# Experts of a routed MLP: steps of 256 tokens with the weights still in layer 1, in place of blocks of 128

## The chip, the cores and the metric

The kernel runs on one core of one Trainium2 chip. The metric is the device time of one execution in microseconds (us), less is better. A profiled execution gives the trace; its times count from the first instruction. PE is TensorE's matmuls, PEld its weight loads, DVE is VectorE, ACT is ScalarE, POOL is GpSimd, SP is SyncE, which issues DMAs.

## The reference

```python
# attention with a memory term, 4 x 8 heads x 576 tokens x 64     -> x (2304, 512)
x = moe(x, w_in, w_out)          # relu(x @ w_in)**2 @ w_out, d_ff 2048
xn, en = x / |x|, emb / |emb|
logits = xn @ en.T / tau         # 8 experts
expert_idx = argmax(logits, axis=1);  gate_w = softmax(logits)[expert_idx]
for e in range(8):
    h = np.maximum(x[mask_e] @ w1[e], 0.0)        # 512 -> 1024
    out[mask_e] = gate_w[mask_e] * (h @ w2[e])    # 1024 -> 512
```

On its inputs the experts 0 to 7 get 466, 171, 106, 0, 676, 436, 0 and 449 tokens, worked out from the reference itself.

## The kernel before

All products are made of three float32r matmuls: each operand is split in a high part (`...h`, an ACT copy) and the rest (`...l`, a DVE subtraction), and hi\*hi + lo\*hi + hi\*lo is summed in PSUM.

The program runs attention, with the first half of the MLP woven in; then the second half of the MLP in 9 chunks of 256 tokens (`Mlp.layer1`: weights still, x moving, 12 matmuls 256 wide; `Mlp.layer2`: 6 matmuls 512 wide; chunks in the order 8, 0, 1, ..., 7). Behind each chunk DVE and PE route its tokens (`Mlp.route`): the expert's number, the rank within the expert (`R.lj`: rank modulo 128 and block number), a one-hot tile `R.L` that POOL makes from the rank. After four chunks `first_block` names the expert with most tokens so far as the first; the experts run in the order 4, 5, 7, 0, 1, 2. It gathers its first 128 tokens, of which the places come from small matmuls into `tab0`, and turns them on PE (`xT0`), so that the experts can begin before the routing is done.

`tables` then works out, on DVE with one row of matmuls on PE (`tab`), the token of each row of each block (`T.idxg`), where to store it (`T.idxs`), and words of bits in `T.meta` by which the engines branch: `odd` (which of two weight buffers a block uses), `change` (the expert changes), `more` (there is another expert to load). Its second part, the gates (norms, an exponential, three products `rg`, and 18 matmuls `tg`), is only needed where results are stored.

`experts` runs blocks of 128 tokens: 18 for sure, up to 25 behind branches; 21 run here. Each has two arms in the code, one for each weight buffer (`Wh[slot]`, `Wl[slot]`). In an arm the order of PE, ACT and DVE is as written:

- `layer1`: x still, 24 matmuls with 512 weights moving; ACT's Relu brings h to SBUF
- `turn_h` twice: 4 PE transposes of h, then hi and lo (`hh`, `hl`)
- `layer2`: 24 matmuls, 512 wide, into `y`; `turn_x`: 4 transposes of the next block's gathered tokens `xg`, then hi and lo
- `own` and `ahead`: pieces of a new expert's weights are split in hi and lo (ACT, DVE), in blocks next to a change of expert
- behind the arm: SP's loads of later weights, POOL's gather for block s + 2, DVE's scaling by the gate, POOL's scatter (`store`)

Of the kernel before, what the change touches and what calls it, by code (L numbers as in the profile page):

```python
# [9 lines left out]
F32 = DT.float32  # L10
F32R = DT.float32r
# [19 lines left out]
NBLK = 25  # L31
NSURE = 18
# [26 lines left out]
TURN0 = 5  # L59
# [554 lines left out]
class Mlp:  # L614
# [158 lines left out]
    def routing(self, c, late, emb, tau):  # L773
# [8 lines left out]
        self.sq = c.tile([128, DM], BF16, name="sq")  # L782
# [18 lines left out]
    def route(self, cc, x2):  # L801
# [51 lines left out]
        V.tensor_reduce(rk, t16, AX.X, ALU.add)  # L853
        ri = c.tile([128, 2, 2], I32, name="ri", tag="ri")
# [17 lines left out]
    def first_block(self):  # L872
# [36 lines left out]
        for sl in spans:  # L909
            V.scalar_tensor_tensor(b0[:, sl], R.lj[:, 1, sl], 0.0, R.O[:, sl, 0], ALU.is_equal, ALU.mult)  # L910
            V.tensor_scalar_mul(rhs[:, sl, 0], b0[:, sl], R.iotap)
            V.tensor_tensor(rhs[:, sl, 1], b0[:, sl], R.iotat[:, sl, 0], ALU.mult)
        tab = R.ps.tile([128, 512], F32, name="tab0", tag="r")
        tiles = [t for sl in spans for t in range(sl.start, sl.stop)]
        for t in tiles:
            nc.tensor.matmul(tab[:, :2], R.L[:, t], rhs[:, t], start=t == tiles[0], stop=t == tiles[-1])
        p1 = c.tile([128, 1], F32, name="p1")
        V.tensor_scalar(p1, tab[:, 0:1], -1.0, None, ALU.add)
        idx = c.tile([128, 1], I32, name="idx0")
        V.scalar_tensor_tensor(idx, tab[:, 1:2], 128.0, p1, ALU.mult, ALU.add)  # L920
        m = len(tiles) * 128
        nc.gpsimd.indirect_dma_start(sh.xg[0], None, sh.x2d[:m], IO(ap=idx, axis=0), bounds_check=m - 1, oob_is_err=False)
        for _ in range(TURN0):
            yield
        pt = self.psr.tile([128, 512], F32, name="xt", tag="xt", bufs=2)
        for kc in range(4):
            nc.tensor.transpose(pt[:, kc * 128:kc * 128 + 128], sh.xg[0][:, kc * 128:kc * 128 + 128], sh.ident)
        sh.xT0 = [c.tile([128, DM], F32R, name=n) for n in ("xT0h", "xT0l")]
        split(nc, pt, *sh.xT0, nc.scalar, nc.vector)
        yield  # L930

# [30 lines left out]
def routing_setup(tc, sh, c):  # L962
# [20 lines left out]
    R.iotat = c.tile([128, NTT, NBLK], BF16, name="iotat")  # L983
    for a, n, base in ((0, NTT - 2, 2), (NTT - 2, 2, 0)):
        nc.gpsimd.iota(R.iotat[:, a:a + n], [[1, n], [0, NBLK]], base=base, channel_multiplier=0,
                       allow_small_or_imprecise_dtypes=True)

    R.two = c.tile([128, NBLK], I32, name="two")
    nc.gpsimd.iota(R.two, [[1, NBLK]], base=126, channel_multiplier=0)
# [8 lines left out]
def tables(ctx, tc, sh):  # L998
# [5 lines left out]
    T.idxg = c.tile([128, NBLK], I32, name="idxg")  # L1004
    T.idxs = c.tile([128, NBLK], I32, name="idxs")
    T.gate = c.tile([128, NBLK], F32, name="gate")
    T.meta = c.tile([128, NBLK + 4], I32, name="meta")
# [7 lines left out]
    V.tensor_scalar(ci, cnt[:, :E], 127.0, None, ALU.add)  # L1015
    V.tensor_scalar(ci, ci, 7, None, ALU.arith_shift_right)
# [4 lines left out]
    for t in cum:  # L1021
# [15 lines left out]
    V.tensor_tensor(sb, sb, R.lj[:, 1], ALU.add)  # L1037
    Bk = st.tile([128, NTT, NBLK], BF16, name="Bk")
    V.tensor_tensor(Bk, R.iota128[:, :NBLK].unsqueeze(1).to_broadcast([128, NTT, NBLK]),
                    sb.unsqueeze(2).to_broadcast([128, NTT, NBLK]), ALU.is_equal)  # L1040
    rg = st.tile([128, NTT, 3, NBLK], BF16, name="rg")
    rhs = rg[:, :, :2]
    V.tensor_scalar_mul(rhs[:, :, 0], Bk, R.iotap)
    V.tensor_tensor(rhs[:, :, 1], Bk, R.iotat, ALU.mult)
    tab = pst.tile([128, 512], F32, name="tab", tag="r")
    for i in range(NTT):
        nc.tensor.matmul(tab[:, :2 * NBLK], R.L[:, i], rhs[:, i].rearrange("p a b -> p (a b)"),
                         start=i == 0, stop=i == NTT - 1)
    P1 = st.tile([128, NBLK], F32, name="P1")
    V.tensor_copy(P1, tab[:, :NBLK])  # L1050
    idx = st.tile([128, NBLK], F32, name="idx")
    V.scalar_tensor_tensor(idx, tab[:, NBLK:2 * NBLK], 128.0, P1, ALU.mult, ALU.add)
    first = V.tensor_scalar(T.idxg, idx, -1.0, 0.0, ALU.add, ALU.max)
    for s in range(1, 2):
        nc.gpsimd.indirect_dma_start(sh.xg[s], None, sh.x2d, IO(ap=T.idxg[:, s:s + 1], axis=0),
                                     bounds_check=NT - 1, oob_is_err=False)
    with tc.issue_after(first.ins):
        ge = st.tile([128, NBLK, E], F32, name="ge")
        V.tensor_tensor(ge, R.iota128[:, :NBLK].unsqueeze(2).to_broadcast([128, NBLK, E]),
                        cend.unsqueeze(1).to_broadcast([128, NBLK, E]), ALU.is_ge)  # L1060
        ex = st.tile([128, NBLK], F32, name="ex")
# [5 lines left out]
        V.tensor_tensor(ge, ge, used.unsqueeze(1).to_broadcast([128, NBLK, E]), ALU.mult)  # L1067
        at = st.tile([128, NBLK], F32, name="at")
# [3 lines left out]
        V.tensor_tensor(ge, at.unsqueeze(2).to_broadcast([128, NBLK, E]), rank.unsqueeze(1).to_broadcast([128, NBLK, E]),  # L1072
                        ALU.is_equal)
        flags = st.tile([128, 3, NBLK], F32, name="flags")
        V.memset(flags[:, :, 0], 0.0)
        more = st.tile([128, NBLK], F32, name="more")
        V.tensor_reduce(more, ge, AX.X, ALU.add)
        V.tensor_tensor(ge, ge, R.iota128[:, :E].unsqueeze(1).to_broadcast([128, NBLK, E]), ALU.mult)
        nx = st.tile([128, NBLK], F32, name="nx")
        V.tensor_reduce(nx, ge, AX.X, ALU.add)  # L1080
        e8 = st.tile([128, NBLK], I32, name="e8")
        V.tensor_scalar(e8, nx, R.e0, None, ALU.add)
        V.tensor_scalar(T.meta[:, :NBLK], e8, E - 1, None, ALU.bitwise_and)
        lt = st.tile([128, NBLK], F32, name="lt")
        V.tensor_scalar(lt, ex, 7.5, None, ALU.is_lt)
        V.tensor_tensor(flags[:, 1, 1:], at[:, 1:], at[:, :NBLK - 1], ALU.not_equal)
# [5 lines left out]
        V.tensor_tensor(flags, flags, R.two.bitcast(F32).unsqueeze(1).to_broadcast([128, 3, NBLK]), ALU.mult)  # L1092
        words = st.tile([128, 4], F32, name="words")
        V.tensor_reduce(words[:, :3], flags, AX.X, ALU.add)
        V.tensor_copy(words[:, 3:], cend[:, E - 1:E])
        last = V.tensor_copy(T.meta[:, NBLK:], words)
        neg = st.tile([128, NBLK], F32, name="neg")
        V.tensor_scalar(neg, idx, 0.0, BIG, ALU.is_equal, ALU.mult)
        wrap = st.tile([128, NBLK], F32, name="wrap")
# [4 lines left out]
    with tc.issue_after(last.ins):  # L1104
# [29 lines left out]
def experts(tc, sh, gates, w1, w2, out):
    nc = tc.nc
    T = sh.T
    with ExitStack() as ctx:
        st = ctx.enter_context(tc.tile_pool(name="est", bufs=1, reuse_waits="tile"))
        psh = [sh.psm.tile([128, 512], F32, name=f"psh{j}", tag="y", bufs=2) for j in range(2)]
        pst = [sh.psm.tile([128, 512], F32, name="pst0", tag="L1", bufs=1)]  # L1140
        pst += [sh.psr.tile([128, 512], F32, name=f"pst{j}", tag="xt", bufs=2) for j in range(1, 3)]
        psy = [sh.psr.tile([128, 512], F32, name=f"psy{j}", tag="y", bufs=2) for j in range(2)]
        ident = sh.ident
# [15 lines left out]
        new_h = ring(1, "h", [128, F], F32)
        new_hh = ring(2, "hh", [128, 512], F32R)  # L1160
        new_hl = ring(2, "hl", [128, 512], F32R)
        spare = sh.x1[NCH - 1].rearrange("p a b -> p (a b)")
        new_psh = ring(2, "psh", None, None, psh)
        new_pst = ring(3, "pst", None, None, pst)
        new_psy = ring(2, "psy", None, None, psy)

        xg, xT, hb = {}, {}, {}

        def gather(s):
            if s >= NBLK:  # L1170
                return
            t = sh.xg[s % 2]
            nc.gpsimd.indirect_dma_start(t, None, sh.x2d, IO(ap=T.idxg[:, s:s + 1], axis=0),  # L1173
                                         bounds_check=NT - 1, oob_is_err=False)
            xg[s] = t

        def turn_x(s):
            if s >= NBLK:
                return
            t = xg.pop(s)  # L1180
            pt = new_pst()
            for kc in range(4):
                nc.tensor.transpose(pt[:, kc * 128:kc * 128 + 128], t[:, kc * 128:kc * 128 + 128], ident)
# [255 lines left out]
```

## Time and profile before

| what | value |
|---|---|
| time, median of 3 runs (lowest to highest) | 978.58 us (978.37 to 980.16) |
| the profiled execution | 976.67 us, of which the span of its instructions is 974.7 us |
| mean granted TensorE clock | 0.982 |
| PE busy | 924.9 us, 95% of the span |
| DVE, ACT, POOL busy | 615.6, 553.8, 278.6 us |

Matmuls overlap: the length of one in a timeline is longer than the distance between the starts of two, and the distance is what a matmul costs. So costs on PE are read from start to start. The expert stage runs from 691.92 us, the first matmul of block 0, to the last matmul at 966.39 us.

### The profile page before, as it was taken

What the parts mean: (1) busy time and instruction counts of PE and PEld (TensorE: products, weight loads), DVE (VectorE), ACT (ScalarE), POOL (GpSimd) and SP (SyncE); (2) the same over time, 40 slices, a digit from 0 to 9 for tenths busy, and PEclk for the clock granted to TensorE, in tenths of its full rate; (3) what the DMA queues carried; (4) which work ended last, traced back from release to release, by engine and by line L of the source; (5) the groups of instructions that cost most, each with busy time, mean ns of one, the idle gap of its engine ahead of it and who ended that gap; (6) DMA issues with size and microseconds to landing.
All of it is one profiled execution on the core that took longest, in us unless ns stands there. A gap on an engine that the chain in (4) does not pass through costs nothing. (4 is left out here: it accounts for less than half of the span.)

```text
span 974.7 us, 19052 instructions
## 1 busy us (share of the span) xinstructions
PE 924.9 (95%) x5864; PEld 772.3 (79%) x5864; DVE 615.6 (63%) x1741; ACT 553.8 (57%) x1425; POOL 278.6 (29%) x346
## 2 busy tenths in 40 slices
PE   7887798899999999999999999999989999999996
PEld 6666675688888888898888988898777878887875
DVE  4797768656676765488517778888642444444364
ACT  4676767677676766576655555664422434444353
POOL 4364554533333443101111112441412111111121
PEclk8999989899999999999999999999999999999998
DMA  6676655454444430254311112421061342425160
GB/s 165 148 177 149 156 138 143 99 127 94 117 95 115 95 85 2 67 171 154 109 44 44 64 46 92 158 66 44 23 218 46 92 154 85 173 73 185 66 204 28
DMA packets 106779, 105.10 MB, mean 108 GB/s; under 512 B 65967, under 2 KB 76207, under 8 KB 106624
## 3 DMA queue, kind: packets, MB, share of 16 engines
q1 hardware_dynamic: 101200, 90.17, 33.2%
q0 software_dynamic: 4224, 12.89, 3.9%
q8 instruction: 58, 0.95, 0.4%
q14 instruction: 97, 0.79, 0.3%
q10 hardware_dynamic: 1200, 0.30, 0.1%
HBM read 70.01 MB, written 14.43 MB: 87 GB/s over the span
## 5 line engine op out<-in xcount | busy, mean ns | idle before, releaser
L680 PE MATMUL ps<-xh,Wh 128*128 128x256 f32 x416 | 119.7, 288 | 0.0
L392 POOL TENSOR_SCALAR A<-A,sm,g 128x512 f32<-128x512 f32 (+4 forms) x108 | 75.4, 706 | 153.3 <-DVE sm L455 60.9
L680 PE MATMUL ps<-xl,Wh 128*128 128x256 f32 x416 | 118.3, 284 | 0.9 <-DVE xl L654 0.9
L680 PE MATMUL ps<-xh,Wl 128*128 128x256 f32 x416 | 118.1, 284 | 0.0
L714 PE MATMUL y<-Wh,gh 128*128 128x512 f32 x288 | 115.3, 400 | 0.1
L716 PE MATMUL y<-Wh,gl 128*128 128x512 f32 x288 | 113.6, 394 | 0.0
L715 PE MATMUL y<-Wl,gh 128*128 128x512 f32 x288 | 113.4, 394 | 0.0
L446 ACT ACTIVATE A<-A,nm 128x256 f32<-128x256 f32 (+2 forms) x144 | 80.3, 558 | 37.8 <-DVE nm L438 36.8
L690 DVE TENSOR_TENSOR gl<-r,gh 128x256 fp32r<-128x256 f32 x144 | 69.5, 483 | 46.2 <-ACT gh L689 41.7
L684 ACT ACTIVATE r<-ps 128x256 f32<-128x256 f32 x144 | 54.8, 380 | 76.5 <-PE ps L680 73.1
L438 DVE CUSTOM_DVE_ANT_0 A<-ps,mask 64x256 f32<-64x256 f32 (+4 forms) x160 | 75.5, 473 | 33.7 <-PE ps L431 30.9
L109 DVE TENSOR_TENSOR hl<-pst,hh 128x512 fp32r<-128x512 f32 x42 | 29.0, 691 | 104.4 <-ACTq L1215 93.6
L680 PEld LDWEIGHTS ps<-xh,Wh 128*128 128x128 f32 x416 | 79.7, 192 | 4.9 <-issue 1.9
L680 PEld LDWEIGHTS ps<-xl,Wh 128*128 128x128 f32 x416 | 79.8, 192 | 3.8 <-DVE xl L654 1.1
L680 PEld LDWEIGHTS ps<-xh,Wl 128*128 128x128 f32 x416 | 79.9, 192 | 0.0
L689 ACT CAST gh<-r 128x256 fp32r<-128x256 f32 x144 | 58.4, 405 | 37.6 <-PE y L715 35.5
L1308 POOL DMA_INDIRECT out_dram<-x,idxs x21 | 21.2, 1011 | 197.1 <-DVE x L1307 149.4
L1250 PE MATMUL psy<-Wh,hh 128*128 128x512 f32 x168 | 70.2, 418 | 0.0
L1252 PE MATMUL psy<-Wh,hl 128*128 128x512 f32 x168 | 66.8, 398 | 0.4 <-DVEq L1215 0.4
L108 ACT CAST Wh<-x 128x512 fp32r<-128x512 f32 x96 | 55.0, 618 | 20.5 <-SPq L1297 7.9
L1251 PE MATMUL psy<-Wl,hh 128*128 128x512 f32 x168 | 66.4, 395 | 0.0
L716 PEld LDWEIGHTS y<-Wh,gl 128*128 128x128 f32 x288 | 54.1, 188 | 13.6 <-DVE gl L690 0.7
(333 smaller groups left out, 2426.6 us busy)
## 6 DMA issues: line engine op xcount, KB each, us to landing
x<-in_moe_w_dram SPq DMA_DIRECT2D x48, 512.0 KB, 3.8
raw<-in_moe_w_in_dram SPq DMA_DIRECT2D x16, 512.0 KB, 4.1
raw<-in_moe_w_out_dram SPq DMA_DIRECT2D x16, 512.0 KB, 4.0
ks<-hk SPq DMA_DIRECT2D x60, 128.0 KB, 2.4
x2d<-x SPq DMA_DIRECT2D x18, 256.0 KB, 2.0
kn<-in_k_dram SPq DMA_DIRECT2D x32, 128.0 KB, 2.8
vn<-in_v_dram SPq DMA_DIRECT2D x32, 128.0 KB, 2.7
x2p<-x SPq DMA_DIRECT2D x16, 256.0 KB, 2.4
```

What stands on the lines that cost most here:

```text
L392: nc.gpsimd.tensor_scalar(A, A, a, b, ALU.mult, ALU.mult)
L438: nc.vector.tensor_tensor_reduce(A[rows, a:n], tiles[j][rows, :w], mask[rows, end - w:end], -1.0, 3e38, ALU.add, ALU.min, nm[rows, j:j + 1])
L446: nc.scalar.activation(A[:, a:a + w], src, AF.Exp, bias=nm[:, 0:1], scale=sign, accum_out=sm[:, i:i + 1])
L680: nc.tensor.matmul(ps[:, :CH], a, b, start=n == 0, stop=n == len(ops) - 1)
L689: self.later(3, "act", lambda: nc.scalar.copy(gh, r))
L690: self.later(3, "dve", lambda: nc.vector.tensor_tensor(gl, r, gh.bitcast(F32), ALU.subtract))
L714: nc.tensor.matmul(y, gh[:, sl], wh, start=first, stop=False)
L715: nc.tensor.matmul(y, gh[:, sl], wl, start=False, stop=False)
L716: nc.tensor.matmul(y, gl[:, sl], wh, start=False, stop=last)
L1250: nc.tensor.matmul(y, hh[:, sl], a, start=n == 0 and kc == 0, stop=False)
L1251: nc.tensor.matmul(y, hh[:, sl], b, start=False, stop=False)
L1252: nc.tensor.matmul(y, hl[:, sl], a, start=False, stop=n == 1 and kc == 3)
```

## The change

- A step of 256 tokens takes the place of two blocks; there are at most 17 steps, 9 for sure. Their tables have 34 columns (halves of steps) where there were 25.
- Layer 1 holds 128 x 128 of the weights still and moves the step's 256 tokens: 96 matmuls 256 wide a step, in four groups `g` of 256 hidden units. Its result comes out turned, so h isn't transposed; ACT makes `hh` from PSUM by Relu and DVE `hl` from PSUM by max and subtraction.
- Layer 2 runs the two halves of 128 tokens apart, each 6 matmuls a group. From step 1 on, the second half stands in a branch that PE alone takes: past it when the step's second half holds no token (a new word of bits, `half`).
- The order in a step: layer 1 of group 0 and 1, layer 2 of 0 and 1, layer 1 of 2 and 3, layer 2 of 2, 8 transposes of the next step's tokens, layer 2 of 3.
- Step 0 needs 256 tokens of the first expert ahead of the tables: `first_block` gathers and turns a second half after 7 chunks (`SEEN`). `R.hole` leaves ranks free if fewer than 256 of them were seen.
- The gates' second part on DVE is issued ahead of step 0 in place of behind block 1, and `sq`, an output that nobody reads, is put in a part of `x1[8]`.

The diff, cut to its core:

```diff
-NBLK = 25
-NSURE = 18
+NST = 17
+NHB = 2 * NST
+NSURE = 9
+SEEN = 7
...
-        self.sq = c.tile([128, DM], BF16, name="sq")
+        self.sq = self.sh.x1[NCH - 1].rearrange("p a b -> p (a b)")[:, DM:2 * DM]
...
         V.tensor_reduce(rk, t16, AX.X, ALU.add)
+        if n >= SEEN:
+            V.scalar_tensor_tensor(rk, O[:, :, 0], R.hole[:, 0:1], rk, ALU.mult, ALU.add)
...
+        fetch(0)
         for _ in range(TURN0):
             yield
...
+        turn(0)
+        while R.count < SEEN:
+            yield
+        cnt = R.ps.tile([128, 512], F32, name="cnt", tag="r")
+        nc.tensor.matmul(cnt[:, :E], R.ones, R.Osum[:, SEEN - 1], start=True, stop=True)
+        V.tensor_scalar(R.hole[:, 0:1], cnt[:, 0:1], -1.0, float(CH), ALU.mult, ALU.add)
+        V.tensor_scalar_max(R.hole[:, 0:1], R.hole[:, 0:1], 0.0)
+        fetch(1)
+        for _ in range(TURN1):
+            yield
+        turn(1)
         yield
...
+            def layer1(g):
+                ps = new_bank().rearrange("p (a b) -> p a b", a=2)
+                for a in range(2):
+                    sl = slice((2 * g + a) * 128, (2 * g + a) * 128 + 128)
+                    for kc in range(4):
+                        for j, (w, x) in enumerate(((Wh, hi), (Wh, lo), (Wl, hi))):
+                            nc.tensor.matmul(ps[:, a], w[kc][:, sl], x[:, kc], start=kc + j == 0, stop=kc + j == 5)
+                hh, hl = hT[g] = new_hh(), new_hl()
+                nc.scalar.activation(hh, ps, AF.Relu)
+                nc.vector.scalar_tensor_tensor(hl, ps, 0.0, hh.bitcast(F32), ALU.max, ALU.subtract)
+
+            def layer2(g):
+                hh, hl = hT[g]
+                for h in range(2):
+                    with tc.If(bit(words["half"], s) < 1) if s and h else nullcontext():
+                        half(g, h, hh, hl)
...
+            own(4)
+            layer1(0)
+            own(5)
+            layer1(1)
+            own(6)
+            layer2(0)
+            own(7)
+            layer2(1)
...
+            ahead(0)
+            layer1(2)
+            ahead(1)
+            layer1(3)
+            ahead(2)
+            layer2(2)
+            if s + 1 < NST:
+                for h in range(2):
+                    turned(nc, sh, pst[h], h)
+            ahead(3)
+            layer2(3)
...
         load(range(8), 0)
...
+        next(gates)
+        block(0)
```

**The order, place 1: PE in an arm.** The first rows are an arm of before, in the middle of its layer 2 (`psy` is y, `pst` a bank for transposes, line 1229 turns h).

```order
L1250 MATMUL psy_9291<-Wh_4_5678,hh_9295 128x512
L1251 MATMUL psy_9291<-Wl_4_5686,hh_9295 128x512
L1252 MATMUL psy_9291<-Wh_4_5678,hl_9297 128x512
L1229 MATMUL pst_9288<-ident,h_9294 128x128 x4
L1250 MATMUL psy_9291<-Wh_5_5679,hh_9295 128x512
```

Here are the rows of the change, in a step's layer 2 of group 2, at the branch around the second half (`psy_9341`).

```order
L1253 COMPARE_AND_BRANCH
L1261 MATMUL psy_9341<-Wh_6_5680,hh_9343 128x512
L1262 MATMUL psy_9341<-Wl_6_5688,hh_9343 128x512
L1263 MATMUL psy_9341<-Wh_6_5680,hl_9345 128x512
L1261 MATMUL psy_9341<-Wh_6_5680,hh_9343 128x512
L1262 MATMUL psy_9341<-Wl_6_5688,hh_9343 128x512
L1263 MATMUL psy_9341<-Wh_6_5680,hl_9345 128x512
L1253 UNCONDITIONAL_BRANCH
L1253 UNCONDITIONAL_BRANCH [waits PE_49]
L961 MATMUL pst_9338<-ident,xg_6592 128x128 [waits DMASW4_49]
```

The transposes of h are gone; the two that end a branch are the end of the body and the way past it, and the way past waits for PE's own work.

**The order, place 2: DVE where the gates' second part stands.** In before that is the end of block 1 (the second of its arms is shown): the lo part of block 2's tokens stands first, the gates (lines 936 and on) behind it:

```order
L109 TENSOR_TENSOR xT0l<-pst_9289,xT0h 128x512
L1221 COMPARE_AND_BRANCH
L109 TENSOR_TENSOR Wl_3_82<-x_3_93,Wh_3_74 128x512
L1221 UNCONDITIONAL_BRANCH x2
L1283 UNCONDITIONAL_BRANCH
L936 TENSOR_SCALAR sq<-ss 128x18
L937 TENSOR_SCALAR sq<-sq 128x18
```

In the change that is the end of step 0. `xTl` is the lo part of step 1's tokens, written in two halves, and the rows around it are the gates:

```order
L1153 CAST gp<-gt 128x18
L1154 TENSOR_TENSOR gr<-gt,gp 128x18
L1159 TENSOR_TENSOR rg<-Bk,gp 128x18x34
L1155 CAST gp<-gr 128x18
L111 TENSOR_TENSOR xTl<-pst_9338,xTh 128x4x128
L1235 COMPARE_AND_BRANCH
L111 TENSOR_TENSOR Wl_3_5685<-x_3_93,Wh_3_5677 128x512 x2
L1235 UNCONDITIONAL_BRANCH x2
L1156 TENSOR_TENSOR gr<-gr,gp 128x18
L1159 TENSOR_TENSOR rg<-Bk,gp 128x18x34
L1157 CAST gp<-gr 128x18
L111 TENSOR_TENSOR xTl<-pst_9339,xTh 128x4x128
```

The gates have moved ahead of both halves of `xTl`, which step 1's second matmul reads.

**The order, place 3: PE in the second half of the MLP, one MLP step after the seventh chunk was routed.** Before:

```order
L680 MATMUL ps<-xh_8736,Wl_0_5682 128x256
L714 MATMUL y<-Wh_7_5681,gh 128x512
L715 MATMUL y<-Wl_7_5689,gh 128x512
L716 MATMUL y<-Wh_7_5681,gl 128x512
L714 MATMUL y<-Wh_7_5681,gh 128x512
```

In the change 14 pairs of a weight load and a matmul into `tab` stand there, of which the first is shown; `L` is the one-hot tile of POOL:

```order
L682 MATMUL ps<-xh_8739,Wl_0_5682 128x256
L716 MATMUL y<-Wh_7_5681,gh 128x512
L717 MATMUL y<-Wl_7_5689,gh 128x512
L926 LDWEIGHTS L
L926 MATMUL tab_8844<-rhs_8043,L 128x2
```

The MLP's third matmul of that group now stands behind those 14.

## Rows read from the trace of the kernel before

**Rows 1.** The page, busy time of PE

```profile
PE 924.9 (95%) x5864; PEld 772.3 (79%) x5864; DVE 615.6 (63%) x1741; ACT 553.8 (57%) x1425; POOL 278.6 (29%) x346
```

**Rows 2.** Windows: length; busy PE, PEld, DVE, ACT, POOL; granted clock, DMA share, GB/s

```profile
691.92:752.49 60.57, 56.72 (x306) 45.07 (x305) 29.15 (x115) 15.28 (x28) 12.37 (x12) 0.97 0.32 111
752.49:966.62 214.13, 212.43 (x1021) 172.51 (x1019) 97.99 (x149) 93.70 (x165) 37.92 (x35) 1.00 0.36 121
...
706.76:710.17 3.41, 1.30 (x8) 1.18 (x9) 2.30 (x10) 0.59 (x1) 1.36 (x2) 1.00 0.58 154
710.17:713.58 3.41, 3.41 (x10) 2.63 (x9) 2.21 (x9) 0.41 (x1) 0.63 (x1) 0.50 0.42 105
```

**Rows 3.** Timeline of PE, block 4: start, length, what

```profile
752.49 0.40 PE L1240 MATMUL psh<-Wh,xT0h 128*128 128x512 f32 x1
...
756.46 0.60 PE L1229 MATMUL pst<-ident,h 128*128 128x128 f32 x4
...
757.13 0.39 PE L1240 MATMUL psh<-Wh,xT0h 128*128 128x512 f32 x1
```

**Rows 4.** Timeline of PE, one step of the MLP's second half

```profile
561.80 0.28 PE L680 MATMUL ps<-Wh,Wh 128*128 128x256 f32 x1
...
563.21 0.40 PE L714 MATMUL y<-Wh,gh 128*128 128x512 f32 x1
...
564.62 0.28 PE L680 MATMUL ps<-Wh,Wh 128*128 128x256 f32 x1
```

**Rows 5.** PE's waits from 740 to 967 us: total, times, longest

```profile
PE pst L1229 <- ACT h L1259: 1.7, 3, 0.8
```

**Rows 6.** PE's waits from 691 to 740 us, the second longest

```profile
PE psh L1240 <- DVE lj L858: 0.8, 1, 0.8
```

**Rows 7.** Timeline, the tables during block 0: PE, then DVE

```profile
697.93 0.18 PE L1013 MATMUL cnt<-Osum,ones 128*128 128x8 bf16 x1
...
703.80 0.61 PE L1047 MATMUL tab<-rg,L 128*128 128x50 bf16 x18
...
708.87 0.66 PE L1183 MATMUL pst<-ident,xg 128*128 128x128 f32 x4 [2.25 <-DMA xg<-x2d,idxg]
...
702.29 0.63 DVE L1039 TENSOR_TENSOR Bk<-iota,sb 128x450 bf16<-128x450 f32 x1
...
704.89 0.18 DVE L1053 TENSOR_SCALAR idxg<-idx 128x25 int32<-128x25 f32 x1
...
712.53 0.17 DVE L1096 CAST meta<-words 128x4 int32<-128x4 f32 x1
```

**Rows 8.** Timeline of DVE, the gates' second part, first and last

```profile
724.65 0.18 DVE L936 TENSOR_SCALAR sq<-ss 128x18 int32<-128x18 int32 x1 [0.34 <-issue]
...
730.25 1.70 DVE L1123 TENSOR_TENSOR rg<-Bk,gp 128x450 bf16<-128x450 bf16 x3
```

**Rows 9.** Timeline, routing of the seventh chunk: PE, and POOL's `L`

```profile
666.16 0.18 PE L845 MATMUL pr<-O,tri 128*128 128x16 bf16 x1 [1.19 <-DVE O L840]
...
668.25 1.18 POOL L860 TENSOR_SCALAR L<-iota,lj 128x128 bf16<-128x128 f32 x2 [2.26 <-DVE lj L858]
```

**Rows 10.** Groups by line from 740 to 960 us, DVE and ACT

```profile
L109 DVE TENSOR_TENSOR hl<-pst,hh 128x512 fp32r<-128x512 f32 x35 | 24.2, 692 | 91.8 <-ACTq L1215 82.8 <-ACT hh L108 8.5 <-issue 0.6
...
L1259 ACT ACTIVATE h<-psh 128x512 f32<-128x512 f32 x18 | 10.8, 598 | 51.7 <-PE psh L1240 46.1 <-issue 5.1 <-ACTq L1221 0.5
```

**Rows 11.** Branches of PE's sequencer: ns min/median/max, first and last start

```profile
L1283 PEldq COMPARE_BRANCH  x2: 68/129/190, 749.6 to 750.0; - x2
...
L1283 PEldq COMPARE_BRANCH  x31: 68/208/358, 710.1 to 951.8; - x31
...
L1334 PEldq COMPARE_BRANCH  x5: 67/73/3432, 925.9 to 968.4; - x5
```

**Rows 12.** Timeline, the end: PE, POOL

```profile
966.39 0.39 PE L1252 MATMUL psy<-Wh,hl 128*128 128x512 f32 x1
...
967.85 1.01 POOL L1308 DMA_INDIRECT out_dram<-x,idxs  x1 [10.16 <-DVE x L1307]
```

More of the change, by code (lines that the diff above doesn't have):

```diff
@@ L56 @@
 STRICT, BUSY = 9, {-5: 14, 0: 12, 2: 6}
-TURN0 = 5
+TURN0, TURN1 = 5, 3
 ONPE = (NCH - 2,)
@@ L917, in first_block, with fetch @@
[L917 to L922, printed above, removed]
+        sh.xT = [c.tile([128, 4, CH], F32R, name=n) for n in ("xTh", "xTl")]
+        def fetch(half):
+            n = R.count - 1
+            spans = [slice(0, 2 * n), slice(NTT - 2, NTT)]
+            for sl in spans:
+                V.scalar_tensor_tensor(b0[:, sl], R.lj[:, 1, sl], float(half), R.O[:, sl, 0], ALU.is_equal, ALU.mult)
+                V.tensor_scalar_mul(rhs[:, sl, 0], b0[:, sl], R.iotap)
+                V.tensor_tensor(rhs[:, sl, 1], b0[:, sl], R.iotat[:, sl], ALU.mult)
+            tab = R.ps.tile([128, 512], F32, name="tab0", tag="r")
+            tiles = [t for sl in spans for t in range(sl.start, sl.stop)]
+            for t in tiles:
+                nc.tensor.matmul(tab[:, :2], R.L[:, t], rhs[:, t], start=t == tiles[0], stop=t == tiles[-1])
+            p1 = c.tile([128, 1], F32, name=f"p1_{half}")
+            V.tensor_scalar(p1, tab[:, 0:1], -1.0, None, ALU.add)
+            at = c.tile([128, 1], F32, name=f"at_{half}")
+            V.scalar_tensor_tensor(at, tab[:, 1:2], 128.0, p1, ALU.mult, ALU.add)
+            idx = c.tile([128, 1], I32, name=f"idx_{half}")
+            V.tensor_scalar_max(idx, at, 0.0)
+            m = len(tiles) * 128
+            nc.gpsimd.indirect_dma_start(sh.xg[half], None, sh.x2d[:m], IO(ap=idx, axis=0), bounds_check=m - 1,
+                                         oob_is_err=False)
@@ L923, in first_block, with turn @@
+        def turn(half):
+            pt = self.psr.tile([128, 512], F32, name="xt", tag="xt", bufs=2)
+            turned(nc, sh, pt, half)
+        fetch(0)
         for _ in range(TURN0):
             yield
[L925 to L928, printed above, removed]
@@ L1053, in tables @@
+    V.tensor_copy(P1, tab[:, :NHB])
+    idx = st.tile([128, NHB], F32, name="idx")
+    V.scalar_tensor_tensor(idx, tab[:, NHB:2 * NHB], 128.0, P1, ALU.mult, ALU.add)
     first = V.tensor_scalar(T.idxg, idx, -1.0, 0.0, ALU.add, ALU.max)
-    for s in range(1, 2):
-        nc.gpsimd.indirect_dma_start(sh.xg[s], None, sh.x2d, IO(ap=T.idxg[:, s:s + 1], axis=0),
+    for n in range(2):
+        nc.gpsimd.indirect_dma_start(sh.xg[n], None, sh.x2d, IO(ap=T.idxg[:, 2 + n:3 + n], axis=0),
                                      bounds_check=NT - 1, oob_is_err=False)
@@ L1278, in block, with arms @@
+            ahead(3)
+            layer2(3)
+        def arms(s, flag, *does):
+            kept = [list(r) for r in rings]
+            with tc.If(bit(words[flag], s) < 1) as cmp, tc.manual_schedule(engines=IN_ORDER | {ENG.PE}):
+                does[0]()
+            for r, was in zip(rings, kept):
+                r[:] = was
+            with cmp.Else(), tc.manual_schedule(engines=IN_ORDER | {ENG.PE}):
+                does[1]()
         def block(s):
-            kept = [list(r) for r in rings], dict(xg), dict(xT)
@@ L1293, in block @@
-            if s + 1 < NBLK:
-                with tc.If(bit(more, s + 1) > 0):
+                body(0, 0)
+                words["odd"] = word(0, [ENG.PE, ENG.Activation, ENG.DVE])
+                words["change"] = word(1, [ENG.Activation, ENG.DVE])
+                words["more"] = word(2, [ENG.SP])
+                words["half"] = word(3, [ENG.PE])
+            else:
+                arms(s, "odd", lambda: body(s, 0), lambda: body(s, 1))
+            if s + 1 < NST:
+                with tc.If(bit(words["more"], s + 1) > 0):
@@ L1315, in experts @@
-        change = word(1, [ENG.Activation, ENG.DVE])
-        more = word(2, [ENG.SP])
-        y = block(0)
+        next(gates)
+        block(0)
         with tc.manual_schedule(engines={ENG.PE, *IN_ORDER}):
-            nc.scalar.copy(room(0), y)
-            y = block(1)
-            nc.scalar.copy(room(1), y)
-            next(gates)
-            odd = word(0, [ENG.PE, ENG.Activation, ENG.DVE])
-            y = block(2)
-            next(gates, None)
-        store(0, room(0))
-        store(1, room(1))
@@ L1334, in experts @@
         with ExitStack() as ifs:
-            for s in range(NSURE, NBLK):
+            for s in range(NSURE, NST):
                 ifs.enter_context(tc.If(nbv > s))
-                store(s, block(s))
+                block(s)
+                store(s, y)
 @with_exitstack
@@ L1404, in tile_kernel @@
             pass
+        for _ in sh.R.first:
+            pass
     gates = tables(ctx, tc, sh)
```

287 lines of the change are left out of this document (107 added, 180 removed).

## Prediction

> **What bounds the kernel.** I read the page first: PE is busy 95% of the span [rows 1], so time can be won where PE does less or waits less, and elsewhere only for a wait of PE. The order before the second half of the MLP is the same in both kernels, so I looked at the expert stage and the MLP chunks just ahead of it. Windows cut the expert stage in two [rows 2]: blocks 0 to 3 took 60.57 us, the other 17 took 214.13 us, 12.6 each. In the latter PE waits 1.7 us in all [rows 5]; it is a stream of matmuls. The timeline gives their price, start to start [rows 3]: 17 matmuls 512 wide from 752.49 to 756.46, 0.234 us each; 4 transposes and the matmul behind them 0.67, so a group of transposes costs 0.44. A block is 48 x 0.234 + 3 x 0.44 = 12.5. In blocks 0 to 3, PE also does routing work and waits: 0.8 us for the load of `once` behind DVE [rows 6], 2.25 us for block 1's gather behind the tables [rows 7], and then the granted clock is at its lower level (0.50) for 3.4 us while PE is busy throughout [rows 2], which costs half of that, 1.7.
>
> **A step.** The new layer 1 has the operands and shape of the MLP's: 12 matmuls 256 wide took 1.41 us, 6 of 512 took 1.41 [rows 4]. So a step has 8 x 1.41 for layer 1, 8 x 1.41 for layer 2, and 8 transposes in a row, 0.8 by 2 x 0.36 and a little behind them: 23.4 us for 256 tokens, where two blocks take 24.9. The whole gain of a step is the 16 transposes of h.
>
> Padding takes some back. The experts' counts (676, 436, 449, 466, 171, 106) make 6+4+4+4+2+1 = 21 blocks, and 3+2+2+2+1+1 = 11 steps. Only the last step (106 tokens) has an empty second half, where PE saves 24 wide matmuls, 5.6 us; its layer 1 moves all 256 columns. That step is 17.7 us, and about 1.8 more, since at each of four skips the sequencer waits for PE's own last matmul (an estimate: the length of a matmul, 0.4, less nothing hidden, four times). Steps 2 to 10: 9 x 23.4 - 5.6 + 1.8 = 206.5 against 214.1: **7.6 us less**. In that I put new waits in these steps at nothing. What hides them: hl(g) has 2.8 us (one group of the next layer 1) and more until layer 2 reads it, and needs 0.60 on ACT and 0.69 on DVE [rows 10]; a piece of new weights in front of it is 2 x 0.69 on DVE, and a step that splits eight pieces has 11 us of them plus 6 us of its own work in 23. Without that cover a step next to a change would lose what before lost, some 0.6, at five changes 3 us.
>
> **Steps 0 and 1.** Step 0 begins like block 0. The routing of the last chunk sets the start up to `cnt`, which I leave at 697.9 [rows 7]. From there PE has layer 1 of group 1, layer 2 of group 0 and six single matmuls until `tab`: 2.8 + 2.8 + 1.1, at 704.7. DVE took 5.9 us from `cnt` to `tab` in before; in the change it has one hl more (0.69), tables 34/25 as wide (Bk 0.63 becomes 0.86, the two behind it gain about as much), and loses an idle half microsecond: 704.7 too. `tab` ends 0.65 later at 705.4, 1.0 after that of before.
>
> Behind it PE has 9 wide matmuls, two groups of layer 1, one of layer 2, the transposes and the last group of layer 2: 2.1 + 5.6 + 2.8 + 0.8 + 2.8 = 14.1, and would begin step 1 at 719.6. The gather is hidden: its tokens were there 4.0 us after `idxg` began [rows 7], the second gather adds one issue, about 1.1, and 10.5 us pass until the transposes. So both waits of before go (0.8 and 2.25).
>
> But DVE gets late. It owes, from `tab`'s end: idxg (0.6), the rest of the tables, 712.7 - 705.1 = 7.6 in before with 1.2 of idle time and two splits of 0.6 inside [rows 7], so about 5 now that most are 17 wide; hl(2); the gates' second part, 724.65 to 731.95 = 7.3 [rows 8], of which the three products cost 0.77 each at 34 columns, one of them behind the last split; the load of `once` (0.6) and four skipped branches (0.3 each); hl(3); and the two halves of xTl, the second of them behind it all. With waits of some half microsecond for ACT's exponential: 0.6 + 5 + 0.5 + 0.7 + 7.1 + 0.6 + 1.2 + 0.7 + 1.4 = 17.8, so 723.2; by going through the instructions one by one I come to 722.8. **PE stands from 719.7 to 722.8, 3.1 us**, at the second matmul of step 1. Bounds: none if DVE overlaps as it does in places (two chains interleaved run at 0.1 an instruction); 5 if each wait is paid. A wait of 2.25 brought the lower clock before, so I add 1.6 for it; bounds 0 and 3.4 (two such stretches). Step 1 then takes 23.4, and `tg` 0.9. Step 2 begins at 722.7 + 23.4 + 1.6 + 0.9 = 748.6 against 752.49: **3.9 us less**.
>
> **The MLP chunk in front.** The second half's places (`tab0`, place 3 of the order) need `L` of the seventh chunk. That was made by POOL at 668.25 to 669.43 [rows 9], and DVE's two instructions for `hole` come before it, about 0.3. PE is at `tab0` some 12 x 0.118 + 2 x 0.234 + 0.3 after `pr` at 666.16: 668.4. It waits there until about 669.8, and the 14 small matmuls, `cnt` and four transposes (0.44) cost 0.9. **2.3 us more**; bounds 0.9 (no wait) and 3.
>
> **The end.** In before the scatter is issued 1.1 us after the last matmul's end [rows 12]. Now two results are scaled (0.7 each) and two scatters issued (1.0 each) behind it: **1.2 us more**, bounds 0 and 2.
>
> **PE's branches.** Ten steps have four branches on PE each, and each step jumps over one arm. Before, a jump over an arm took the sequencer 0.07 to 0.36 us [rows 11], and nothing of it reached PE: the sequencer was at block 3's end at 749.6, 2.9 us before block 4's first matmul [rows 3, 11]. An arm had 60 matmuls, now it has 152. The last branch of before, over four blocks of two arms, took 3.43 us [rows 11]. I take 0.5 us for all, and 0 to 34 (ten jumps of 3.43) as bounds, the row of jumps over one arm being far nearer.
>
> [...]
>
> **Sum.** 7.6 + 3.9 - 2.3 - 1.2 - 0.5 = 7.5 us less than the profiled 976.67, which is 1.9 below the median of the runs; on that median 978.58 - 7.5 = 971. A difference of 0.2%, 2 us, is about what this measurement can tell.
>
> **Rivals.**
> - *DVE isn't late, or the clock holds.* For it: half of my chain are short instructions that overlap. Against it: the order of place 2. It gives back 3 to 5 us: 966. Chance 0.15.
> - *The skips don't work and waits come back.* The empty half is one of 22; were it not skipped, 3.8 us, and with new waits next to the changes of expert (3) the rest of the gain is gone: 978. Against it: the changes had 1.7 us of waits [rows 5] with four splits in a row, now two. Between forecast and that, or within 2 us of 978.6: 0.24, half of it within.
> - *Jumps reach PE* (the other side). At each step PE's sequencer stands 3.43 us, and its lead of 2.9 is used up by four branches in a step: each about 0.1 to compare and 0.2 to 0.3 to jump back. Then up to 3.4 us of ten steps show: 971 + 34 = 1005 at most. It decides from 0.75 us a step, 7.5 in all; with half of the lead gone it is 2 us a step: 991. For it: the 3.43 us row. Against it: the lead is made anew in each group of wide matmuls. Chance 0.13.
> [...]
>
> **Numbers.** Forecast 971, its own range 967 to 975, chance 0.48. The range for 8 in 10 takes in the second and half of the third case: 964 to 981. Faster by more than 0.2%: 0.48 + 0.15 + 0.12 = 0.75; same 0.12; slower 0.13.
>
> **What the next profile shows.** Right: step to step 23.4 us without idle PE from step 2 on; no gather wait in step 0; PE idle about 3 us at the first layer 1 of step 1 with xTl's subtraction as the one that ends it, and a lower clock behind it; PE idle over 1 us at `tab0`. Wrong: idle PE or longer spacing at line 1253's branches or at each step's start (jumps); idle PE at layer 2 for hl in steps 2 to 10; steps far from 23.4, which would mean that matmuls 256 wide cost more here than in the MLP.

## The result and the profile after

The changed kernel takes **984.34 us** (median of 12 runs, 982.62 to 990.59) against 978.48 us of before, timed beside it (12 runs, 977.35 to 980.16): a ratio of 1.0069, 95% interval 1.0052 to 1.0087. It is slower; the forecast was 971, so 13.3 us are missing. The profiled execution took 984.24 us, its span 982.5.

Windows, cut at the first matmul of each step, show where (columns as in [rows 2]):

```profile
696.02:723.81 27.79, 27.20 (x201) 24.63 (x199) 21.34 (x101) 6.42 (x13) 10.27 (x9) 1.00 0.39 137
723.81:749.39 25.58, 24.27 (x171) 21.80 (x170) 6.29 (x11) 4.06 (x7) 0.02 (x1) 1.00 0.21 81
749.39:774.88 25.49, 23.42 (x157) 21.05 (x154) 13.13 (x23) 8.34 (x16) 8.56 (x9) 1.00 0.48 149
774.88:798.86 23.98, 23.71 (x153) 21.12 (x153) 9.18 (x15) 7.08 (x13) 4.25 (x4) 1.00 0.42 136
...
822.39:845.55 23.16, 23.16 (x153) 21.15 (x152) 10.43 (x17) 7.70 (x14) 4.09 (x4) 1.00 0.47 160
845.55:870.80 25.25, 23.34 (x153) 20.97 (x152) 11.77 (x18) 8.26 (x16) 4.28 (x5) 1.00 0.39 122
...
918.39:946.16 27.77, 23.32 (x154) 20.96 (x152) 17.83 (x29) 12.88 (x24) 5.31 (x5) 0.97 0.49 157
946.16:967.60 21.44, 20.99 (x128) 18.76 (x128) 7.40 (x12) 6.56 (x12) 2.10 (x3) 0.87 0.02 6
```

PE's busy time in a full step is the 23.4 us of the forecast. But some steps are longer than that: 25.49, 25.25, 27.77. The list of PE's waits from 600 us on (in total, times, longest) gives no clear culprit:

```profile
PE psh L1245 <- issue: 7.0, 4, 4.4
PE psh L1245 <- ACT Wh L110: 2.1, 1, 2.1
PE pr L847 <- DVE O L842: 1.8, 2, 1.2
PE psh L1245 <- DVE xTl L111: 1.3, 1, 1.3
PE tab L926 <- POOL L L864: 0.3, 1, 0.3
```

"issue" means that nothing in the profile held the matmul back. The 2.1 for ACT's `Wh` is of the same kind, at the same place in another step. The timeline has both ahead of the first matmul of layer 1, here of steps 3 and 10:

```profile
772.41 0.39 PE L1263 MATMUL psy<-Wh,hl 128*128 128x512 f32 x1
774.88 0.38 PE L1245 MATMUL psh<-xTh,Wh 128*128 128x256 f32 x1 [2.07 <-ACT Wh L110]
...
941.32 0.39 PE L1263 MATMUL psy<-Wh,hl 128*128 128x512 f32 x1
946.16 0.58 PE L1245 MATMUL psh<-xTh,Wh 128*128 128x256 f32 x1 [4.45 <-issue]
```

The answer to [rows 11] is in the branches of PE's sequencer. L1290 is the choice between a step's two arms, L1253 the branch around a second half (ns min/median/max, first and last start):

```profile
L1290 PEldq COMPARE_BRANCH  x10: 68/1740/4928, 722.1 to 942.1; - x10
...
L1253 PEldq COMPARE_BRANCH  x76: 65/173/382, 730.0 to 965.4; - x76
```

Of the ten choices of an arm, five took 0.07 to 0.09 us. The other five are those of steps 3, 4, 7, 8 and 10, the five that use the second weight buffer and jump over the first arm: 4.93, 3.39, 4.71, 3.45 and 3.97 us. Before step 3 the branch begins at 769.89 and ends at 774.82, and PE's next matmul starts at 774.88; idle time is 4.93 less the 2.9 us by which the sequencer was ahead. The five idle times are 2.07, 0.27, 1.91, 0.33 and 4.45: **9.0 us**. Step 10 has the most, because 3.3 us pass between two records of the sequencer (938.6 and 941.9) just before its branch: there the jump over the second arm, which ends step 9's arm, must lie, of which the profile has no record. Behind step 1's arm there is such a gap too (745.5 to 748.6), which PE's queued work hid.

The last step is also 2.5 us longer than its matmuls cost (21.2 between its first and last matmul; 18.7 in a kernel below without jumps). Windows behind the idle time have the clock at 0.50 first and at 0.70 after that:

```profile
946.10:949.50 3.40, 3.34 (x15) 3.35 (x16) 0.00 (x0) 0.00 (x0) 0.99 (x1) 0.50 0.09 31
949.50:952.90 3.40, 3.40 (x23) 3.40 (x22) 0.54 (x1) 1.17 (x3) 0.00 (x0) 0.70 0.00 0
```

And the end is longer. From the last matmul's start to the end of the span [rows 12] has 974.7 - 966.4 = 8.3 us; here it is 982.5 - 967.4 = 15.1. The timelines of DVE and POOL, and two rows of POOL's sequencer (its closing instruction at L1338, and the drain behind it):

```profile
968.09 1.41 DVE L1320 TENSOR_SCALAR x<-psy,gate 128x512 f32<-128x512 f32 x2 [0.23 <-DVEq L1235]
...
969.78 1.03 POOL L1321 DMA_INDIRECT out_dram<-x,idxs  x1 [1.21 <-DVE x L1320]
973.29 0.99 POOL L1321 DMA_INDIRECT out_dram<-x,idxs  x1 [2.48 <-DMA out_dram<-x,idxs]
...
L1338 POOLq INC_SWDGE_SEM  x1: 1320/1320/1320, 975.5 to 975.5; - x1
...
L1442 POOLq DRAIN  x3: 46/103/4648, 977.1 to 982.3; - x3
```

The second scatter does not follow the first: it waits 2.48 us for the first one's transfer. POOL's closing instruction then comes only 1.2 us behind its end. In before that instruction began at 968.0, inside the only scatter.

### The profile page after: what moved, and what is told of

It reads as the page before. It is cut to its first block, busy times and chain, and to the rows that moved or that the text cites. A ratio compares the mean times of both kernels' runs of the same rounds, so it can differ in the third digit from the quotient of the medians.

```text
span 982.5 us, 19092 instructions
## 1 busy us (share of the span) xinstructions
PE 918.9 (94%) x6271; PEld 791.1 (81%) x6271; DVE 618.4 (63%) x1761; ACT 529.6 (54%) x1387; POOL 282.4 (29%) x351
## 3 DMA queue, kind: packets, MB, share of 16 engines
q8 instruction: 65, 1.06, 0.5%
## 5 line engine op out<-in xcount | busy, mean ns | idle before, releaser
L1245 PE MATMUL psh<-xTh,Wh 128*128 128x256 f32 x352 | 100.8, 286 | 9.2 <-issue 7.0
L1247 ACT ACTIVATE hh<-psh 128x512 fp32r<-128x512 f32 x44 | 26.3, 599 | 147.6 <-PE psh L1245 117.2
L1245 PE MATMUL psh<-xTl,Wh 128*128 128x256 f32 x352 | 99.8, 284 | 1.3 <-DVE xTl L111 1.3
L1245 PE MATMUL psh<-xTh,Wl 128*128 128x256 f32 x352 | 99.8, 283 | 0.0
L1248 DVE SCALAR_TENSOR_TENSOR hl<-psh,hh 128x512 fp32r<-128x512 f32 x44 | 30.4, 690 | 108.7 <-ACT hh L1247 49.5
L1245 PEld LDWEIGHTS psh<-xTh,Wh 128*128 128x128 f32 x352 | 67.4, 192 | 12.4 <-issue 9.2
L1245 PEld LDWEIGHTS psh<-xTl,Wh 128*128 128x128 f32 x352 | 67.3, 191 | 2.2 <-DVE xTl L111 1.6
```

What stands on the lines that cost most here:

```text
L1245: nc.tensor.matmul(ps[:, a], w[kc][:, sl], x[:, kc], start=kc + j == 0, stop=kc + j == 5)
L1248: nc.vector.scalar_tensor_tensor(hl, ps, 0.0, hh.bitcast(F32), ALU.max, ALU.subtract)
```

## The experiments

Each kernel is the changed one with the edit shown, cut to its core; ratios are to before.

**The jumps.** Two theories: the sequencer's jumps cost the idle time (J), or the new weights do, as one row of the waits says (W). The first kernel takes the jumps away, the second cuts them in half.

```diff
-                arms(s, "odd", lambda: body(s, 0), lambda: body(s, 1))
+                with tc.manual_schedule(engines=IN_ORDER | {ENG.PE}):
+                    body(s, SLOT[s])       # 0,0,0,1,1,0,0,1,1,0,1
```

> Every step from 1 on is written once, for the weight buffer that it uses on these inputs, so no step jumps over an arm of the other buffer; all else is the change. Theory J (jumps): the 9.0 us in which PE stands ahead of the first matmul of steps 3, 4, 7, 8 and 10 are its sequencer's jumps over an arm, and the lower clock behind the last of them costs some 2.6 more; both go: 984.3 - 11.6 = 972.7, and no start of a step has over 0.3 us of idle PE. Rival W (weights): PE waits there for a new expert's weights, as the list of waits names ACT's Wh for 2.1 us of it, the same on these inputs without the jumps: the starts of steps 3 and 7 keep their 2 us each and step 10 its 4.4: 982 to 984.

```diff
-                arms(s, "odd", lambda: body(s, 0), lambda: body(s, 1))
+                for p in range(2):         # layer 1 and 2 of groups 0, 1; the rest
+                    arms(s, "odd", lambda: body(s, 0, (p,)), lambda: body(s, 1, (p,)))
```

> Each step's two arms are cut in two: a choice of buffer ahead of layer 1 of group 0 and another ahead of layer 1 of group 2, so that an arm has 72 or 80 matmuls in place of 152; there are twice as many jumps, each over half the distance. Theory J, in the form that the distance makes a jump slow: an arm of 60 matmuls in the kernel before was jumped in 0.07 to 0.36 us, so these are short too and hidden: 973 to 974. Rival J2 (each taken jump costs some us whatever its distance, and only the lead of the sequencer hid it in the kernel before): twice as many jumps show, over 990. Rival W: 984.

Without jumps: 974.07 us, ratio 0.9943 (0.9926 to 0.9959). With twice as many of half the length: 973.69, 0.9942 (0.9927 to 0.9958). Both are some 10 us faster than the change, as J says and W and J2 don't. The list of PE's waits from 640 us on of the kernel without jumps, and the choice of an arm in the kernel with short ones:

```profile
PE pr L848 <- DVE O L843: 1.8, 2, 1.2
PE psh L1246 <- DVE xTl L112: 1.3, 1, 1.3
PE tab L927 <- POOL L L865: 0.3, 1, 0.3
```

```profile
L1293 PEldq COMPARE_BRANCH  x20: 71/154/3722, 723.0 to 947.4; - x20
```

"issue" and ACT's `Wh` are gone from the first: the weights were never late. In the second 18 of 20 branches took 0.36 us or less. The two that stay slow (3.12 and 3.72) are at the changes from the first to the second buffer ahead of steps 3 and 7, where the jump over the 80 matmuls of one arm is followed at once by one over the next 72. At the third such change, ahead of step 10, the choice took 0.22.

**Is a slow jump one to code that is not loaded?**

```diff
+            if 0 < s and s + 1 < NST:      # in the middle of a step
+                tc.mark_branch_hint_location(f"arm{s + 1}", 1 - bit(words["odd"], s + 1), engines=[ENG.PE])
```

> The change with its arms whole, and one instruction more on PE in the middle of each step, which tells the sequencer whether the jump into the next step's second arm will be taken. Theory J, in the form that a slow jump is one whose target is not yet loaded: the target is loaded ahead, the jumps of 3.4 to 4.9 us become short and the 9.0 us of idle PE go, some of it kept where the jump over the second arm at the end of a step, which has no such instruction, is slow too (step 10, 1 to 3 us): 973 to 977. Rival: a slow jump is not a matter of loading (the sequencer works through what it passes, or the hint does nothing): 984 and the same five slow jumps.

979.32 us, 1.0008 (0.9995 to 1.0021): half of the loss is back, short of what was expected. Its PE waits under "issue":

```profile
PE psh L1245 <- issue: 5.0, 4, 2.0
```

The branches of steps 4 and 8 fell from 3.4 to under 0.5 us, and step 10's idle time from 4.45 to 0.75. Those of steps 3 and 7 stayed at 4.8 and 4.7, and one branch around a second half became slow (3.28), without a wait of PE. So telling the sequencer of the target helps where the step before ran in the second arm, and mostly doesn't where the sequencer jumps over the second arm in between. Why not there stays open: ahead of step 3's choice queue 8, of which more below, makes as many transfers in step 2 with the hint (at 750.62 and 765.30) as without (750.12 and 766.04).

That a slow jump goes with a load of instructions, the record of the DMA transfers shows more directly. Queue 8, whose kind the profile calls `instruction`, moves blocks of 16 KiB (65 of them in the change, 1.06 MB), and they go with PE: from 464 to 678 us in the change, where PE has no branches, 232 to 266 of PE's matmuls and weight loads lie between two of them. The windows of the change around the slow choices of steps 3, 4 and 10 (769.8:774.9, 795.3:798.9, 941:946.2) have one block each:

```profile
q8 instruction: 1, 0.02, 1.3%
...
q8 instruction: 1, 0.02, 1.6%
...
q8 instruction: 1, 0.02, 1.2%
```

In the traces of all thirteen kernels, each of the 38 branches of PE's sequencer of over 1 us holds the start of such a transfer, and 4 of the 1144 shorter ones do (7 of 7 and 2 of 127 in those of before and of the change); the gaps of the change behind steps 1 and 9 hold one too (746.23, 939.14). The hint moved it: for step 4 it started at 796.40, 1.0 us into the branch, and with the hint at 793.88, 2.6 ahead of the branch; for step 8 at 892.36 in the branch, and at 887.09, 5.0 ahead of it.

So each slow jump has its load; the arm that it passes is, with 152 matmuls and their weight loads, 304 instructions. How many instructions are held ready, and which, no run shows.

**Arms in four, and the gates.** One kernel moves the gates' second part alone, from ahead of step 0 into the middle of step 1, on top of the two-part arms:

```diff
-        next(gates)
         block(0)
...
                 for p in range(2):
+                    if s == 1 and p == 1:
+                        next(gates)
```

> As e2_split, with the gates' second part issued on DVE between the two parts of step 1 in place of ahead of step 0. If PE's 1.3 us at step 1's second matmul is only the lateness that the gates bring to xTl, it goes, and the 7 us of gates lie in DVE's idle time between hl(1) and hl(2): 973.7 - 1.3 = 972.4. Rival: hl(2) and hl(3) of step 1, or the tg matmuls behind it, come late in their turn and PE waits there for 1 us or more: 973.5 or above.

972.93, 0.9944 (0.9928 to 0.9959), not to be told from the two-part kernel's 973.69 by the times. In the profiles step 1 took 25.58 and now 24.02, PE busy throughout, and the wait for `xTl` is off the list. The edit does in its place what was expected; the size is below what these runs resolve.

**The end.** The scalings in order, and no wait between the two scatters, which write different rows:

```diff
+            with tc.manual_schedule(engines={ENG.DVE}):
...
+                    if first is not None:
+                        tc.declare_no_dep(d.ins, first.ins, reason="other rows of out")
```

> DVE scales the first half's result ahead of the second's, and the second half's scatter no longer waits for the first half's to land (their rows of the output are different ones). Theory S (scatters in a row): from the last matmul's start to the end the change took 15.1 us where before took 8.3; 2.2 of it are the wait of the second scatter for the first, 0.7 the order of the two scalings: 984.3 - 2.9 = 981.4. Rival: the end is set by the landing of the last transfer and the checks behind it however the two scatters lie, and only 0.7 or less comes back: 983.6 or more.

984.24, 1.0062 (1.0044 to 1.0080): no gain in the times. In the profile the scatters now follow each other, and from the last matmul to the end it is 13.1 us in place of 15.1:

```profile
971.04 1.03 POOL L1323 DMA_INDIRECT out_dram<-x,idxs  x1 [0.56 <-DVE x L1322]
972.37 0.99 POOL L1323 DMA_INDIRECT out_dram<-x,idxs  x1 [0.30 <-DMA xg<-x2d,idxg]
```

But step 3 took 25.74 us here, 1.8 more than in the profile after; behind an idle time of 1.89 the clock was at 0.72 and then 0.78, behind 2.07 in the profile after at 1.00:

```profile
774.84:778.24 3.40, 3.40 (x21) 3.40 (x22) 1.29 (x2) 0.69 (x2) 1.46 (x2) 0.72 0.65 237
778.24:781.64 3.40, 3.40 (x25) 3.40 (x24) 1.79 (x3) 1.63 (x3) 0.00 (x0) 0.78 0.21 51
```

So the same edit was put on the two-part arms, where the idle time is nearly gone.

> The arms in two parts as in e2_split, and the end as in e4_tail. In e4_tail the profile's end (last matmul to the end of the span) came out 2.0 us shorter than the change's, but its median did not move, and its step 3 shows a lower clock for some 7 us behind the idle time at its start. Theory S+C: the end is worth 2.0 us, and in e4_tail this was lost in the noise of the clock behind the idle steps; with the idle time gone it shows: 973.7 - 2.0 = 971.7. Rival: the end is worth nothing by the time of a run, since that does not count the same end: 973.7.

972.57, 0.9941 (0.9923 to 0.9960): 1.1 us below the two-part kernel, between the two expectations and within the intervals. The profile's end fell from 15.2 to 13.4; that the time of a run falls as much is not shown. All three edits together, with the arms in four parts:

> The end as in e4_tail, the gates as in f2_gates, and the arms cut in four (48, 24, 48 and 32 matmuls). By theory J the two slow jumps that e2_split still has (3.1 and 3.7 us, at the changes from the first to the second weight buffer, where two jumps of 80 and 72 matmuls follow each other) become short, and 1.0 us of idle PE at the starts of steps 3 and 7 goes: 973.7 - 2.0 - 1.3 - 1.0 = 969.4. Rival: four choices a step each cost something on PE (0.2 us a choice would be 6 us in all): 975.

**968.72, 0.9904 (0.9887 to 0.9920)**: faster than before and than the change by 10 and 15.6 us, and 5.0 less than the two-part kernel. No choice of an arm took over 0.45 us. Its steps 2 to 10, and the same of the change:

```profile
745.89:951.88 205.99, 205.00 (x1348) 185.73 (x1345) 99.78 (x157) 74.18 (x134) 41.58 (x40) 1.00 0.41 129
```

```profile
749.39:967.60 218.21, 208.73 (x1348) 187.75 (x1345) 99.04 (x157) 73.38 (x134) 41.16 (x40) 0.98 0.38 122
```

205.99 is what the prediction had for them (206.5). Yet 13.3 us from the last matmul to the end stay, 5.0 more than before. First I held the second half's scaling and scatter to be the cause. The next kernel leaves these out in the eleventh step, where they write nothing:

```diff
-                for h in range(2):
+                for h in range(1 if s == 10 else 2):
```

> As f4_best, but the eleventh step (the last on these inputs, with an empty second half) scales and scatters its first half alone; the second scatter writes no row there. f4_best's profile has 13.3 us from the last matmul to the end, before had 8.3. Theory: what is left of that is the second half's scaling (0.7), its scatter (1.3) and POOL's wait for a landing behind it (some 2) ahead of POOL's closing work: without them 13.3 - 2 to 4, so 965 to 967. Rival: the closing wait is for any scatter of the last step, so that only 1.3 goes: 967.4, and the rest stays unexplained.

968.04, 0.9885 (0.9865 to 0.9904), the end 12.7 us. The theory falls: 0.6 of 5.0. POOL's closing instruction shows what is left; it begins 3.2 us behind the last scatter's start (954.75) in the four-part kernel, and 4.1 behind it (955.95) with one scatter less:

```profile
L1350 POOLq INC_SWDGE_SEM  x1: 1320/1320/1320, 958.0 to 958.0; - x1
```

```profile
L1350 POOLq INC_SWDGE_SEM  x1: 1300/1300/1300, 960.0 to 960.0; - x1
```

The order tells what it waits for. Where the branches leave out steps, POOL makes up for the transfers that these would have issued, on each of the eight semaphores (DMASW0 to 7) that its transfers take in turn. In before, with four blocks left out, the row at which it enters is the first of these; in the change, with six steps left out, the second:

```
L1334 ISA [waits DMASW5_49,DMASW6_49,DMASW4_49,DMASW7_49,DMASW1_49,DMASW0_49]
L1338 ISA [waits DMASW4_49,DMASW5_49,DMASW3_49,DMASW6_49,DMASW2_49,DMASW7_49,DMASW1_49,DMASW0_49]
```

Before's last scatter has DMASW3, which is not waited for; that is so by the count of blocks alone. With eight waited for, all transfers of the last step must land first: its scatters, and the gathers of tokens for a step that doesn't run. In the four-part kernel the waits run from 955.0 to 957.9:

```profile
L1350 POOLq EVENT_SEMAPHORE  x4: 17/43/43, 955.0 to 957.9; - x4
```

The second gather lands at 957.06, the last scatter at 957.85. So without a scatter no more than 0.8 could go, and 0.6 went. The test leaves one step out in place of six (the code of steps 12 to 16, which don't run here, is left out of the kernel):

```diff
-            for s in range(NSURE, NST):
+            for s in range(NSURE, 12):
```

> As f4_best, with the code of 12 steps in place of 17 (11 run on these inputs), so that one step is left out at the end in place of six. In the order of f4_best, POOL's closing instruction behind the last step waits for all eight lanes of its transfers, those of the last step's scatters among them, since the six steps that are left out would have used them all; in before it waits for six of the eight, and the last scatter's is not among them. Here it waits for four, of the step before the last. Theory L (lanes): POOL's closing work then begins 0.6 us behind the last scatter's issue, as in before, in place of 3.7: 13.3 us from the last matmul to the end become 10.2 and the time 968.7 - 3.1 = 965.6. Rival: POOL's closing work waits for the landing in any case: 968.7, or a little less for a shorter last jump of PE.

**965.66, 0.9861 (0.9841 to 0.9882)**, and the end is 9.9 us. POOL's timeline and its closing instruction:

```profile
957.42 1.03 POOL L1331 DMA_INDIRECT out_dram<-x,idxs  x1 [0.55 <-DVE x L1330]
958.75 1.00 POOL L1331 DMA_INDIRECT out_dram<-x,idxs  x1 [0.31 <-issue]
...
L1350 POOLq EVENT_SEMAPHORE  x2: 17/30/43, 958.0 to 958.1; - x2
L1350 POOLq INC_SWDGE_SEM  x1: 1310/1310/1310, 958.2 to 958.2; - x1
```

It now begins ahead of the last scatter, and its waits take 0.1 us. The theory of the semaphores gave the number.

**What the skip of an empty half is worth.** Tried twice, with PE always running the second half.

```diff
-                    with tc.If(bit(words["half"], s) < 1) if s and h else nullcontext():
+                    with nullcontext():
```

> PE has no branch around the second half in layer 2 and always runs it, on these inputs in the last step only to no use. If a skip saves what it leaves out, 24 matmuls of 0.23 us, less the four places where PE's sequencer waits for PE's own last matmul (spacing 0.55 in place of 0.23, 1.3 us in all), this is 4.3 us slower than the change: 988.6. If the branches cost more elsewhere (the arms get 8 branches shorter, and the sequencer comes to the end of a step with more of a lead), it is 986 or less.

On the change: 993.77, 1.0161 (1.0141 to 1.0181), 9.4 slower where 4.3 were expected. The profile shows where: the jumps fell out otherwise, with one choice of 6.21 us (that this comes of the shorter arms is argued, not shown). Idle time is 3.3 at step 3, 3.3 at step 7 and 4.8 at step 10, 2.3 more in all. Behind step 3's the clock was at 0.70 and 0.79 in two windows of 3.4 us, some 1.7 more; the 1.5 that are left, beside the skip's own 3.9 (below), are inside the intervals. ACT is named for 6.6 of the idle time, which was the jumps':

```profile
PE psh L1245 <- ACT Wh L110: 6.6, 2, 3.3
PE psh L1245 <- issue: 4.8, 1, 4.8
```

On the four-part kernel the edit stands alone:

> As f4_best, without PE's branch around the second half in layer 2, which is always run. Here no step waits for a jump, so the branch's own worth shows, which in e3_noskip was mixed with other jumps: the last step takes 24 matmuls of 0.23 us more (5.6), less three places where the skip had a spacing of 0.55 and one of 1.09 in place of 0.12 to 0.23 (1.7): 968.7 + 3.9 = 972.6. Rival: without the branches the sequencer is further ahead and other steps gain too, or the branches cost each step something that the spacing hides: 971 or less.

973.09, 0.9943 (0.9926 to 0.9961): 4.4 us slower than with the skip, and the last step takes 23.43 in place of 19.51. By the step's length the skip saves 3.9 us, as worked out.

## Why the prediction was wrong, step by step

In the profiles, term by term (before's profile was 1.9 below its median, after's at it):

| stretch | forecast | measured |
|---|---|---|
| up to step 0 | +2.3 | +4.1 |
| steps 0 and 1 | -3.9 | -7.2 |
| steps 2 to 10, with the jumps | -7.1 | +4.1 |
| the end | +1.2 | +6.9 |
| sum | -7.5 | +7.9 |

- **PE's branches, 0.5 us forecast, is the step that failed.** They cost 9.0 us of idle time and 2.5 of lower clock. The rival "Jumps reach PE", to which I gave 0.13, was right that they do, but not in how: it had ten jumps of 3.43 us and a lead of 2.9 that a step's four branches use up. Seven of ten were slow (five choices, and the two gaps behind steps 1 and 9), at 3.1 to 4.9 us, and the lead was still 2.8 to 3.1, so that 9.0 us came through of them. I priced a jump over 152 matmuls by the nearest row, one over 60, though the only far jump in the trace took 3.43. It was also not seen that a jump out of one arm and one over the next follow each other.
- **The end, 1.2 us forecast, failed next**: 6.9. I counted the second scaling and scatter, and neither the wait between the scatters (2.2; the profile of the edited end shows it, the times of its runs do not) nor POOL's closing wait for the landing of the last step's gathers and scatters (3.1, shown by the kernel of 12 steps).
- **A step at 23.4 us, and the skip**, held: 206.0 for steps 2 to 10 in the kernel with short jumps against 206.5. No wait of PE for `hl` or for weights came up.
- **Steps 0 and 1** came out better by 3.3. Step 0 took 27.79, as forecast (27.7). DVE was late with `xTl`, for the reason given, but by 1.3 us in place of 3.1; in the timeline its two halves and the gates' products overlap. The lower clock that I added (1.6) did not come in this profile (1.00 over step 1).
- **The MLP chunk**: `tab` waits 0.3 where I had 1.4, since the seventh chunk's `L` was nearly there. From the seventh `pr` to step 0 the change lost 1.8 against 2.3. The other 2.3 us of the table's first row were there already at that `pr` (668.43, in before 666.16 [rows 9]), behind code that is the same in both up to it but for a few small instructions. In the profiles of the other kernels step 0 starts anywhere from 694.1 to 698.1 us. So I take this part as how one execution differs from another; before has one profile, so it is not shown.

The sum closes on the medians too: 971, and 8.5 for the jumps, 2.5 for the clock, 5.7 for the end, less 3.3 for steps 0 and 1 and 0.5 for the chunk, is 983.9 against 984.3.

## What to carry to other kernels

Before code behind a branch grows, count the instructions of an arm on the busiest engine, and take a jump's price from the trace's far jumps (here 3.43 us), not from the many short ones (0.07 to 0.36): short arms more often can be cheaper than long ones once (here 973.69 us with the arms in two parts, 984.34 with whole ones). Look at two jumps that follow each other as one (argued from the two slow choices of the two-part arms). At the end of a kernel, ask of each transfer what waits for it to land: here that cost 3.1 us.

## What the runs showed of the hardware

- A jump of PE's sequencer over an arm of 24 to 80 matmuls took 0.07 to 0.45 us. Over 152, seven of ten were slow in the change, at 3.1 to 4.9 us, and so were two of three over 80 and 72 in a row (3.1 and 3.7); each slow one had the start of a transfer of 16 KiB of queue 8 (`instruction`) in it. In the change PE had 2.8 to 3.1 us of work ahead of the slow choices. An instruction that names the target in advance made two of five slow choices short (3.4 to under 0.5 us).
- Behind idle times of 2 us the clock fell in one run (0.72 and 0.78 behind 1.89) and not in another (1.00 behind 2.07); behind 4.4 it was at 0.50 for over 3 us. It also fell without a jump: in the profile of the kernel without jumps step 0 took 30.7 us in place of 27.8, with the clock at 0.62 from 703 to 710 us, behind a wait of 0.6 that the change has there too, at 1.00. Over their runs the four kernels with slow jumps at whole arms spread by 4.4 to 8.0 us, the others by 2.2 to 5.2; how much of that is the clock is not shown.
- At its end POOL waited for the landing of transfers whose semaphores the left-out steps would have used: 13.3 us from the last matmul to the end with six steps left out, 9.9 with one.
- The profile's releaser of a wait was plainly wrong in two runs: "ACT Wh" stood for 2.1 and 6.6 us of waits that were jumps.
